# Top-32 attention with an MLP on one Trainium2 core: the smaller halves of the late score rows made by GpSimd as an integer difference

## The chip, the cores and the metric

The kernel runs on one core of one Trainium2 chip. That core has five instruction queues that matter here: TensorE (PE, matrix products), VectorE (DVE), ScalarE (ACT), GpSimd (POOL) and SyncE (SP, which issues the transfers). Each queue runs its instructions in the order in which the program put them; between queues there are only semaphores. The metric is the device time of one execution in microseconds (us).

## What is computed

Attention in which each query keeps only its 32 largest scores, followed by a layer norm and a two-layer MLP with a residual. Cut to what matters:

```python
# batch 8, heads 8, sequence 576, head size 64; all float32
scores = scale * np.matmul(q, k.transpose(0, 1, 3, 2))
kth = np.partition(scores, -32, axis=-1)[..., -32:-31]
scores = np.where(scores >= kth, scores, -1e9)
attn = softmax(scores)
x = heads_joined(np.matmul(attn, v))            # (8, 576, 512)
xn = (x - mean(x)) / np.sqrt(var(x) + 1e-6) * g_ln
out = x + np.maximum(xn @ w_ch1, 0.0) @ w_ch2   # 512 -> 2048 -> 512
```

## The kernel before

**Units.** The score rows are worked off in 160 units, numbered from 0. A whole unit has 128 queries of two heads: a tile `sc` of 128 partitions by two rows of 576 scores. There are 128 whole units. The other 32, called rest units, hold the last 64 queries of two heads in one row of 576.

**Finding the 32nd largest score of a row.** VectorE's MAX8 gives the eight largest of a row, and MATCH_REPLACE8 overwrites those eight, so four rounds give the threshold. To make these rounds shorter, `halve` (lines 442 to 457) first folds the row of 576 into two of 288: `hi` has the larger, `lo` the smaller of each pair (a score and the one 288 places further). Both were made by VectorE, in one TENSOR_TENSOR each (lines 456 and 457). `select` (line 459) then runs four rounds, 0 to 3, on `hi`; at the start of round 1 it takes the eight largest of `lo` (line 470) and puts them beside `hi`, so that rounds 2 and 3 also see them (296 elements). If more than eight of a row's 32 come out of `lo`, that is not enough: GpSimd's small subtraction in `watch` (line 497) records what is needed to notice it, and a second pass of the whole kernel would follow. It does not run with these inputs.

**What follows a unit.** `prepare` and `mask` (lines 486 and 524): ScalarE scales the threshold (line 490), makes a steep ramp of the row (RELU, line 527), and GpSimd subtracts the scores from it (line 530); the exponential on ScalarE (line 538) then gives zero outside of the 32. The weights are turned, for most units by VectorE's transpose (line 572) and a round trip through HBM, for others by PE (line 601), and PE multiplies them by the values (line 664). The MLP's products (lines 821, 860, 981) are cut into small items and handed out between these steps so that PE has work all the time. For most row blocks the second layer uses a seven-product scheme; its sums and differences are made by GpSimd (lines 911 to 917), as are the joins of its parts (961, 965), the residual (789) and the centring for the layer norm (743, 746).

**The order.** It is written out by hand in one loop over steps `n` (line 1265). In step `n` the current unit `u` is unit `n`, `nxt` is unit `n+1` and `mk` is unit `n-1`. In order of the code, a step does: scores of unit `n+2` on PE, masks of `mk` and its watch, the copy of the scores of `n+2` from PSUM (line 414), round 0 of `u`, MLP items, round 1 of `u` (with line 470), the transpose of unit `n-2`, rounds 2 and 3 of `u`, and last `halve(nxt)`. The calls `fill()` between them hand out MLP items, and with them the sums, joins and residuals that are due on GpSimd.

**Buffers.** `lo` has one buffer (`lopool`, line 70). `hi` has two fixed homes (line 110), taken in turn. `sc` has five. The first steps also convert the MLP's weights from their 64-bit form, on ScalarE, GpSimd and VectorE; `CONVERTING` (line 1103) is the last step of that, 21.

Of the kernel before, what the change touches and what calls it, by code (L numbers as in the profile page):

```python
# [10 lines left out]
ALU = mybir.AluOpType  # L11
FP32 = mybir.dt.float32
U32 = mybir.dt.uint32
# [16 lines left out]
def compute(  # L30
# [12 lines left out]
    nc = tc.nc  # L43
    P = nc.NUM_PARTITIONS
# [12 lines left out]
    def pool(name, bufs, **kw):  # L57
        return ctx.enter_context(tc.tile_pool(name=name, bufs=bufs, **kw))
# [3 lines left out]
    HALF = S // 2  # L62
# [7 lines left out]
    lopool = pool("lo", 1)  # L70
# [23 lines left out]
    def brief(name):  # L94

        return psps.tile([P, 512], FP32, tag="ps", name=name)
# [345 lines left out]
    def halve(u):  # L442

        nt = len(u.tiles)
        u.lo = lopool.tile([P, 2, HALF], FP32, tag="lo", name="lo")  # L450
        u.hi = hi_homes[u.i % 2]
        sides = int(doubt is not None)
        u.low, u.body = (sides * LOWS + HALF, sides * LOWS) if doubt is None or u.i // 2 % 2 else (0, LOWS)
        a, b = u.sc[:, 0:nt, 0:HALF], u.sc[:, 0:nt, HALF:S]
        lo, hi = u.lo[:, 0:nt], u.hi[:, 0:nt, u.body : u.body + HALF]
        nc.vector.tensor_tensor(hi, a, b, ALU.max)  # L456
        nc.vector.tensor_tensor(lo, a, b, ALU.min)  # L457

    def select(u, i):

# [25 lines left out]
    def prepare(u):  # L486

        nt = len(u.tiles)
        u.bias, u.edge = u.top[:, 0:nt, 0], u.thr[:, 0:nt, 6]
        nc.scalar.mul(u.edge, u.thr[:, 0:nt, 7], STEEP)  # L490
        nc.scalar.mul(u.bias, u.bias, -scale)

    def watch(u):

        nt = len(u.tiles)
        half, c = u.i // 16 % 2, 1 + 2 * (u.i % 16)
        nc.gpsimd.tensor_tensor(
            watched[:, half, c : c + nt], u.hi[:, 0:nt, u.low + 7], u.thr[:, 0:nt, 7], ALU.subtract
        )
        if u.i % 16 == 15 or u.i == N - 1:  # L500
            u.ends_watch = True
            u.half = half
# [21 lines left out]
    def mask(u, t):  # L524
        if u.e is None:
            u.e = epool.tile([P, 2, S], FP32, tag="e", name="e")
        nc.scalar.activation(  # L527
            u.e[:, t], u.sc[:, t], AF.Relu, bias=u.edge[:, t : t + 1], scale=-STEEP
        )
        nc.gpsimd.tensor_tensor(u.e[:, t], u.e[:, t], u.sc[:, t], ALU.subtract)  # L530
# [21 lines left out]
    def heads_of(g, h, i0, i1):  # L552
        c0 = h * (J + 1)
        return g.pt[:, i0:i1, c0 : c0 + J]

    def ends_of(g, i0, i1):
        return g.pt[:, i0:i1, J]
# [101 lines left out]
    def values(g):  # L659
        vb = g.job.v  # L660
        av = brief("av")
        for c in range(J):
            for h in range(2):
                nc.tensor.matmul(  # L664
                    av[h * D : (h + 1) * D, 0 : g.nq],
                    vb[:, h * (J + 1) + c, :],
                    heads_of(g, h, 0, g.nq // 32)[:, :, c],
                    start=(c == 0),
                    stop=False,
                )  # L670
        for h in range(2):
            nc.tensor.matmul(  # L672
                av[h * D : (h + 1) * D, 0 : g.nq],
                ends[:, h * D : (h + 1) * D],
                ends_of(g, 0, g.nq // 32),
                start=False, stop=True,
            )
        g.av = av
# [345 lines left out]
    def form_pair(i, part):  # L1024

        lo, hi = slice(2 * i, 2 * i + 2), slice(NF // 2 + 2 * i, NF // 2 + 2 * i + 2)
        b11, b12 = w2[:, lo, 0 : 2 * P], w2[:, lo, 2 * P : DM]
        b21, b22 = w2[:, hi, 0 : 2 * P], w2[:, hi, 2 * P : DM]  # L1030
        tt = nc.gpsimd.tensor_tensor
        t1, t2 = wt[:, 0, lo], wt[:, 1, lo]
        if part == 0:
            tt(t1, b12, b11, ALU.subtract)
            tt(t2, b22, t1, ALU.subtract)
            return
        x = xpool.tile([P, 2, DM], FP32, tag="x", name="form")
        t4, t3 = (x[:, s].rearrange("p (f n) -> p f n", f=2) for s in range(2))
        tt(t3, t2, b11, ALU.subtract)
        tt(t4, b21, t2, ALU.subtract)  # L1040
        return i, x

    def keep_pair(made):
        i, x = made
        for s in range(2):
            nc.sync.dma_start(scratch[:, s, i], x[:, s])
        if i == 3:
            kept_forms[0] = now[0]
# [54 lines left out]
    CONVERTING = max(n for n in batches if batches[n]) + 2  # L1103
# [26 lines left out]
    for j in jobs:  # L1130
        if j.hp == NHP - 1:
            b = j.b
# [26 lines left out]
    def at(i):  # L1159
        return units[i] if 0 <= i < N else None  # L1160
# [96 lines left out]
    take_scores(units[0])  # L1257
    load(fresh[1], nc.sync, nc.scalar)
    halve(units[0])
    scores(units[1])  # L1260
    take_scores(units[1])
# [3 lines left out]
    for n in range(END):  # L1265
# [8 lines left out]
        u, nxt, mk = at(n), at(n + 1), at(n - 1)  # L1274
# [14 lines left out]
            scores(x)  # L1289
        if g and not quick:  # L1290
            values(g)
        if mk:
            prepare(mk)
            for t in range(len(mk.tiles)):
                mask(mk, t)
        if mk and doubt is not None:
            watch(mk)
        if all(map(done, ready)):
            if made_pair:
                keep_pair(made_pair.pop())  # L1300
            if pairs_left:
                made = form_pair(*pairs_left.pop(0))
                made_pair.extend([made] if made else [])
            if None not in (kept_forms[0], plain_done[0]) and formed[0] is None:
                formed[0] = n
# [93 lines left out]
        if nxt:  # L1399
            halve(nxt)  # L1400
# [30 lines left out]
@with_exitstack  # L1431
def kernel(
    ctx: ExitStack,
    tc: tile.TileContext,
    *operands: bass.AP,
):
    nc = tc.nc
    doubt = ctx.enter_context(tc.tile_pool(name="doubt", bufs=1)).tile(
        [1, 1], I32, tag="doubt", name="doubt"
    )  # L1440
    compute(tc, *operands, low_rounds=1, doubt=doubt[:])
    again = nc.values_load(
        doubt[:], min_val=0, max_val=1,
        skip_runtime_bounds_check_because="a comparison's result",
    )
    with tc.If(again > 0):
        compute(tc, *operands, low_rounds=2, doubt=None)
# [31 lines left out]
```

## Time and profile before

| What | us |
|---|---|
| Median of three executions (lowest, highest) | 1563.04 (1561.82, 1563.74) |
| The profiled execution's own time | 1566.49 |
| Span of its instructions in the profile | 1564.6 |

The profile is of one execution, 3.45 us above the median. In it, "busy" is the time in which an engine executes; a wait is put down to what ended it. Instructions that have no record of their own time, such as issuing a transfer, are not counted as busy. PE's products are pipelined and their ends are modelled, so a PE that is busy all the time may still not be at its highest rate. The "chain that ended last" is found by going back from the last instruction to what released each one.

### The profile page before, as it was taken

Reading aid. Unit: us, or ns where it says so; the run is one execution under the profiler, and the core shown is the slowest. Engines: PE = TensorE matmul, PEld = TensorE weight load, DVE = VectorE, ACT = ScalarE, POOL = GpSimd, SP = SyncE. Lnnn points to the kernel's source line nnn. Section 1 sums busy time; section 2 is a strip of 40 time slices with the busy share of each in tenths; the row PEclk is TensorE's granted clock in tenths of the full one; section 3 lists DMA queues with packets and bytes.
Section 4 is the critical chain, followed back from the end, with each engine's and each line's share of the span. In section 5 each row is a group of like instructions: output and inputs, shape, how many; then the busy total and the mean of one; then the engine's idle time right before and its main releaser. Section 6 shows DMA issues by size and latency. Waiting matters only on the chain.

```text
span 1564.6 us, 27256 instructions
## 1 busy us (share of the span) xinstructions
PE 1467.7 (94%) x8046; PEld 1108.0 (71%) x8046; DVE 1349.1 (86%) x3873; ACT 1075.5 (69%) x3085; POOL 941.2 (60%) x1302
## 2 busy tenths in 40 slices
PE   3678889999999899999999999999999999999997
PEld 2456447576787677778777777777777777788886
DVE  6998899899889998989988999999999999767000
ACT  5988777786777767777777776867677776554421
POOL 4757776756474666656656556565647475737524
PEclk7789989999999999999999999999999999999998
DMA  6634541567648774686744796666667567464511
GB/s 174 165 100 122 143 114 60 151 157 209 177 127 201 192 204 130 180 207 151 222 119 133 183 225 183 159 171 182 187 173 197 173 173 196 118 173 114 151 35 50
DMA packets 374776, 245.62 MB, mean 157 GB/s; under 512 B 255956, under 2 KB 343512, under 8 KB 374616
## 3 DMA queue, kind: packets, MB, share of 16 engines
q1 hardware_dynamic: 371048, 243.17, 57.9%
q8 instruction: 67, 1.10, 0.3%
q10 hardware_dynamic: 3568, 0.59, 0.3%
q14 instruction: 93, 0.76, 0.2%
HBM read 166.14 MB, written 77.53 MB: 156 GB/s over the span
## 4 chain that ended last, share of the span: by engine, by line
PE 52%; DVE 31%; ACT 5%; DMA 5%; POOL 4%; issue 2%; SPq 1%; DVEq 0%; POOLq 0%; ACTq 0%
PE hps L821 21%; PE ops L981 13%; DVE m L478 10%; DVE hi L464 8%; PE scps L433 6%; PE av L664 5%; DVE sc L572 3%; DVE lo L457 2%; DVE hi L456 2%; PE ops L860 2%; DVE hi L470 2%; PE tp L601 2%; POOL e L530 2%; DMA raw<-in_moe_w_ch_dram 1%; PE av L672 1%
## 5 line engine op out<-in xcount | busy, mean ns | idle before, releaser
L530 POOL TENSOR_TENSOR e<-e,sc 128x576 f32<-128x576 f32 x288 | 408.7, 1437 | 492.6 <-ACT e L527 437.7
L821 PE MATMUL hps<-xT,w 128*128 128x256 f32 x2304 | 542.0, 384 | 1.6 <-ACT xT L781 1.6
L821 PEld LDWEIGHTS hps<-xT,w 128*128 128x128 f32 x2304 | 423.4, 191 | 80.8 <-issue 25.9
L478 DVE MAX8 m<-hi 128x8 f32<-128x296 f32 (+1 forms) x1152 | 472.8, 446 | 1.2
L464 DVE MATCH_REPLACE8 hi<-m,hi 128x288 f32<-128x288 f32 (+1 forms) x864 | 378.0, 443 | 0.0
L981 PE MATMUL ops<-w,h 128*128 128x256 f32 x1280 | 306.9, 385 | 1.3 <-ACT o L946 1.3
L981 PEld LDWEIGHTS ops<-w,h 128*128 128x128 f32 x1280 | 235.0, 191 | 44.8 <-issue 13.4
L414 ACT COPY sc<-scps 128x288 f32<-128x288 f32 x576 | 189.1, 402 | 76.8 <-POOL e L530 56.0
L538 ACT ACTIVATE e<-e,m 128x576 f32<-128x576 f32 x288 | 225.4, 785 | 7.8 <-POOL e L530 5.8
L527 ACT ACTIVATE e<-sc,m 128x576 f32<-128x576 f32 x288 | 209.3, 769 | 0.0
L572 DVE STREAM_TRANSPOSE sc<-e 128x1152 f32<-128x1152 f32 x87 | 119.0, 1367 | 52.7 <-ACT e L538 46.2
L844 ACT ACTIVATE h<-hps 128x512 f32<-128x512 f32 x144 | 86.7, 602 | 111.0 <-PE hps L821 110.4
L664 PE MATMUL av<-pt,vb 128*64 128x256 f32 (+2 forms) x1280 | 150.8, 379 | 9.6 <-DMA pt<-turned 6.2
L664 PEld LDWEIGHTS av<-pt,vb 128*64 128x64 f32 x1280 | 82.2, 142 | 69.6 <-issue 20.7
L456 DVE TENSOR_TENSOR hi<-sc 128x576 f32<-128x576 f32 (+1 forms) x160 | 127.0, 794 | 3.0 <-ACT sc L414 3.0
L457 DVE TENSOR_TENSOR lo<-sc 128x576 f32<-128x576 f32 (+1 forms) x160 | 126.9, 793 | 0.0
L433 PE MATMUL scps<-kT,late_qT 64*128 64x288 f32 (+3 forms) x832 | 119.9, 407 | 0.0
L981 PE MATMUL ops<-wt,s 128*128 128x256 f32 x512 | 119.4, 383 | 0.0
L433 PE MATMUL scps<-kT,qT 64*128 64x288 f32 x512 | 95.1, 465 | 24.6 <-ACT pt L613 9.0
L470 DVE MAX8 hi<-lo 128x8 f32<-128x288 f32 x288 | 117.8, 445 | 0.0
L981 PEld LDWEIGHTS ops<-wt,s 128*128 128x128 f32 x512 | 94.7, 190 | 17.3 <-issue 4.1
L433 PEld LDWEIGHTS scps<-kT,late_qT 64*128 64x128 f32 (+1 forms) x832 | 69.0, 166 | 50.0 <-issue 20.2
(108 smaller groups left out, 1747.2 us busy)
## 6 DMA issues: line engine op xcount, KB each, us to landing
turned<-sc SPq DMA_DIRECT2D x87, 576.0 KB, 4.3
pt<-turned SPq DMA_DIRECT2D x348, 144.0 KB, 3.1
w<-forms SPq DMA_DIRECT2D x128, 256.0 KB, 4.8
vb<-in_v_dram SPq DMA_DIRECT2D x80, 288.0 KB, 4.3
raw<-in_moe_w_ch_dram SPq DMA_DIRECT2D x32, 512.0 KB, 4.7
kT<-kept SPq DMA_DIRECT2D x48, 288.0 KB, 3.8
kept<-kT SPq DMA_DIRECT2D x32, 288.0 KB, 3.7
kqin<-in_k_dram SPq DMA_DIRECT2D x116, 72.0 KB, 2.7
```

The lines of the kernel that those rows point to most:

```text
L414: nc.scalar.copy(u.sc[:, t, s * HALF : (s + 1) * HALF], u.made[s][t][:, 0:HALF])
L433: nc.tensor.matmul(ps[i * R : i * R + ql, o : o + width], qT[r, q0 : q0 + ql], kT[r, k0 : k0 + width], start=True, stop=True,)
L456: nc.vector.tensor_tensor(hi, a, b, ALU.max)
L464: nc.vector.match_replace(x, m[:, t, :], x, LOWEST)
L478: nc.vector.max(m[:, t, :], u.hi[:, t, r0 : r0 + width])
L527: nc.scalar.activation(u.e[:, t], u.sc[:, t], AF.Relu, bias=u.edge[:, t : t + 1], scale=-STEEP)
L530: nc.gpsimd.tensor_tensor(u.e[:, t], u.e[:, t], u.sc[:, t], ALU.subtract)
L538: nc.scalar.activation(u.e[:, t], u.e[:, t], AF.Exp, bias=u.bias[:, t : t + 1], scale=-scale, accum_out=g.den[:, col : col + 1],)
L572: nc.vector.transpose(blocks.rearrange("p (j c n) -> p j c n", j=ni, n=32), u.e[:].rearrange("p t n -> p (t n)").rearrange("p (c j k) -> p ...
L664: nc.tensor.matmul(av[h * D : (h + 1) * D, 0 : g.nq], vb[:, h * (J + 1) + c, :], heads_of(g, h, 0, g.nq // 32)[:, :, c], start=(c == 0), s ...
L821: nc.tensor.matmul(ps[0][:, side * N : (side + 1) * N], w1[:, c, f * P : (f + 1) * P], self.xT[:, c, 0:N], start=(c == 0), stop=(c == NC - 1),
L981: nc.tensor.matmul(bank[name][:, 0:Q], a(j), rhs, start=first and j == 0, stop=(j == G - 1), skip_group_check=not first,)
```

## The change

For whole units after step `CONVERTING`, that is unit 22 (the 23rd) and later, `halve` no longer makes `lo`. GpSimd makes it in two integer instructions on the bits of the scores: first the sum of the bits of both halves (`both_halves`), then that sum less the bits of the larger half (`less_larger`). Addition and subtraction wrap around at 32 bits, so what is left are the bits of the smaller half exactly. There are 106 such units. Rest units and the first 22 units are made as before.

In a step, `less_larger(u)` stands on GpSimd's queue ahead of the masks of `mk`, and `both_halves(nxt)` behind the watch of `mk`. The larger half stays on VectorE at the end of the step before.

```diff
@@ halve
         nt = len(u.tiles)
-        u.lo = lopool.tile([P, 2, HALF], FP32, tag="lo", name="lo")
+        if not by_difference(u):
+            u.lo = lopool.tile([P, 2, HALF], FP32, tag="lo", name="lo")
...
         nc.vector.tensor_tensor(hi, a, b, ALU.max)
-        nc.vector.tensor_tensor(lo, a, b, ALU.min)
+        if not by_difference(u):
+            nc.vector.tensor_tensor(lo, a, b, ALU.min)
+
+    def by_difference(u):
+
+        return doubt is not None and not u.rest and u.i > CONVERTING
+
+    def both_halves(u):
+
+        u.lo = lopool.tile([P, 2, HALF], FP32, tag="lo", name="lo")
+        a, b = (u.sc[:, :, c : c + HALF].bitcast(U32) for c in (0, HALF))
+        nc.gpsimd.tensor_tensor(u.lo[:].bitcast(U32), a, b, ALU.add)
+
+    def less_larger(u):
+
+        lo = u.lo[:].bitcast(U32)
+        hi = u.hi[:, :, u.body : u.body + HALF].bitcast(U32)
+        nc.gpsimd.tensor_tensor(lo, lo, hi, ALU.subtract)
@@ the loop over steps
         if g and not quick:
             values(g)
+        if u and by_difference(u):
+            less_larger(u)
         if mk:
             prepare(mk)
             for t in range(len(mk.tiles)):
                 mask(mk, t)
         if mk and doubt is not None:
             watch(mk)
+        if nxt and by_difference(nxt):
+            both_halves(nxt)
```

## Prediction

> **What bounds the kernel now.** I read the page first: the busy time of the engines, the chain that ended last, and the costliest groups.
>
> ```profile
> span 1564.6 us, 27256 instructions
> PE 1467.7 (94%) x8046; PEld 1108.0 (71%) x8046; DVE 1349.1 (86%) x3873; ACT 1075.5 (69%) x3085; POOL 941.2 (60%) x1302
> ...
> PE 52%; DVE 31%; ACT 5%; DMA 5%; POOL 4%; issue 2%; SPq 1%; DVEq 0%; POOLq 0%; ACTq 0%
> ```
>
> TensorE (PE) and VectorE (DVE) share the chain, and GpSimd (POOL) stands far behind. An average over stages can hide what limits each, so next comes the busy time in three stretches (columns: window, its length, then busy time and instructions of PE, PEld, DVE, ACT and POOL, the granted clock, DMA).
>
> ```profile
> 0.00:300.00 300.00, 235.21 (x1137) 152.11 (x1138) 262.33 (x766) 234.16 (x629) 200.84 (x212) 0.89 0.47 124
> 300.00:1300.00 1000.00, 982.30 (x5646) 748.06 (x5645) 966.44 (x2786) 731.44 (x2166) 603.65 (x876) 0.99 0.67 177
> 1300.00:1565.00 265.00, 250.15 (x1267) 207.82 (x1265) 120.32 (x324) 109.92 (x292) 136.67 (x216) 0.98 0.42 118
> ```
>
> In the 1000 us from 300 to 1300, PE is busy for 982 and DVE for 966: two full engines, and each hands work to the other within about one unit. Time taken off DVE alone can therefore be refused by PE. POOL has 396 us idle there. After 1300 PE alone carries the time. What the change touches in the long stretch (groups by line and shape):
>
> ```profile
> L530 POOL TENSOR_TENSOR e<-e,sc 128x576 f32<-128x576 f32 x208 | 294.9, 1435 | 359.3 <-ACT e L527 309.3 <-PE scps L433 21.7 <-DVE m L478 17.5
> L457 DVE TENSOR_TENSOR lo<-sc 128x576 f32<-128x576 f32 x88 | 73.1, 830 | 0.0
> L456 DVE TENSOR_TENSOR hi<-sc 128x576 f32<-128x576 f32 x88 | 73.0, 829 | 0.0
> L821 PE MATMUL hps<-xT,w 128*128 128x256 f32 x1536 | 363.9, 383 | 0.0
> L981 PE MATMUL ops<-w,h 128*128 128x256 f32 x946 | 230.6, 386 | 1.3 <-ACT o L946 1.3
> L981 PE MATMUL ops<-wt,s 128*128 128x256 f32 x384 | 90.5, 383 | 0.0
> ```
>
> POOL's idle time stands almost wholly in front of the mask subtraction (L530), where it waits for ScalarE (ACT). So POOL is idle at the start of a step and does the rest of its queue after the masks.
>
> **What is removed.** 106 of the 160 units are whole and come from the 23rd on; 88 of them lie in the long stretch. DVE loses one minimum (L457) for each: 73.1 us there. How much of it the kernel can use depends on PE. PE leaves 1000 - 982 = 18 us, the least that it can give. What it could give beyond that, were its matrix products packed, is bounded by the rate of the chain's last long run:
>
> ```profile
> 1501.64 27.63 PE hps L821 x128
> ```
>
> 27.63 / 128 = 0.216 us each, so the 2866 such products (1536 + 946 + 384) need 619 us, where they are credited with 363.9 + 230.6 + 90.5 = 685: another 66 us at most. The relief lies between 18 and 73 us. I take 40, near the middle, because most steps have such products to pack, but in small groups between other work.
>
> **What is added, and its price.** GpSimd gets two integer instructions of 128x576 per unit: the sum of both halves (both_halves), and that sum less the larger half (less_larger). The trace has no such instruction at this size. The nearest rows are the float subtraction of the same size (1435 ns above) and GpSimd's integer addition of 128x512:
>
> ```profile
> L178 POOL TENSOR_TENSOR w<-wt 128x512 uint32<-128x512 uint32 x20 | 25.1, 1277 | 0.0
> L178 POOL TENSOR_TENSOR w<-size,wt 128x512 uint32<-128x512 uint32 x12 | 17.8, 1492 | 3.5 <-DVE size L172 3.5
> ```
>
> Scaled by 576/512 these give 1.44 and 1.68 us. I take 1.41, one undisturbed float subtraction (its row is shown below), as the lower integer row agrees with it; the upper end is 1.68. So 88 x 2 x 1.41 = 248 us enter a stretch with 396 idle: POOL goes from 604 to some 852 of 1000. It has room on average. What matters is when. The next rows are one whole step on DVE, from one larger half to the next, and then POOL in the step after it.
>
> ```profile
> 377.85 1.16 DVE L457 TENSOR_TENSOR lo<-sc 128x576 f32<-128x576 f32 x1
> 378.94 0.81 DVE L478 MAX8 m<-hi 128x8 f32<-128x288 f32 x2
> ...
> 380.15 0.44 DVE L464 MATCH_REPLACE8 hi<-m,hi 128x288 f32<-128x288 f32 x1
> 380.51 0.80 DVE L470 MAX8 hi<-lo 128x8 f32<-128x288 f32 x2
> ...
> 385.15 0.73 DVE L456 TENSOR_TENSOR hi<-sc 128x576 f32<-128x576 f32 x1
> 385.81 0.74 DVE L457 TENSOR_TENSOR lo<-sc 128x576 f32<-128x576 f32 x1
> ...
> 388.06 0.80 DVE L470 MAX8 hi<-lo 128x8 f32<-128x288 f32 x2
> ...
> 394.02 0.73 DVE L456 TENSOR_TENSOR hi<-sc 128x576 f32<-128x576 f32 x1
> ```
>
> ```profile
> 386.76 2.78 POOL L530 TENSOR_TENSOR e<-e,sc 128x576 f32<-128x576 f32 x2 [3.59 <-ACT e L527]
> 389.50 0.20 POOL L497 TENSOR_TENSOR watched<-hi,m 128x2 f32<-128x2 f32 x1
> 389.65 3.36 POOL L917 TENSOR_TENSOR h<-h,s 128x128 f32<-128x128 f32 x8
> 393.09 0.19 POOL L756 TENSOR_SCALAR rstd<-mv 128x2 f32<-128x2 f32 x1
> 393.37 0.71 POOL L759 TENSOR_TENSOR rstd<-rstd,columns 128x2 f32<-128x2 f32 x1
> ```
>
> The new waits. In the changed order POOL issues, in each step: less_larger, the two masks, the watch, both_halves for the next unit, and only then the rest (sums of the hidden rows, residuals, centring). less_larger waits for L456; DVE's L470, which picks the eight largest of lo, waits for less_larger; both_halves waits for that L470, as lo has one buffer. Between the end of L456 and L470 DVE has two MAX8 and two replacements: 380.51 - 378.94 = 1.57 us. One GpSimd instruction of 1.41 plus two handshakes just fits. A wait of zero holds only while POOL is free at that moment; each microsecond by which it is late, DVE stands still, with the rest of the selection, the moves (L572) and the next larger half queued behind.
>
> In the step shown POOL has 2.78 + 0.20 + 3.36 + 0.19 + 0.71 = 7.2 us of work. With 2.8 more it is 10.0, against a DVE step of 394.02 - 385.15 = 8.87 less 0.66 (385.81 - 385.15, the pitch of the two halves). So here POOL arrives 1.8 us late. I went through the 88 whole units in this way: POOL's instructions per step as the changed program orders them, with the durations of these rows, against DVE's own work in that step, lateness carried over. In 29 of them POOL is over 0.2 us late, and the lateness sums to 52 us; the steps are those with a burst of eight L917, with two triples of sums, with a residual, or the first whole unit after the short remainder units. PE sets about half of the chain, and lateness in those places costs nothing: the low end is 26. With 1.68 us for each instruction there are 88 x 2 x 0.27 = 48 us more of POOL work, so the high end is about 100. I take 40: most late steps are short ones in which DVE has no slack.
>
> **The shared read of VectorE and GpSimd.** Two rows, one of each engine, show that L456 can wait for a GpSimd instruction:
>
> ```profile
> 800.67 1.41 POOL L530 TENSOR_TENSOR e<-e,sc 128x576 f32<-128x576 f32 x1 [5.67 <-PE scps L433]
> 800.86 1.84 DVE L456 TENSOR_TENSOR hi<-sc 128x576 f32<-128x576 f32 x1
> ```
>
> The clean larger half takes 0.73; here it starts 0.19 after the mask and takes 1.84, so it ended only after the mask had. On average 0.83 - 0.73 = 0.10 us per half are lost so. The change takes one of two such halves away and makes POOL busier at the other: 88 x 0.10 = 9 us gone (inside the 73), about as much more at L456, which I cost at nothing; the ends are 9 us either way. The Trainium skill ("SBUF — State Buffer", section "Who interferes with whom") says that a DVE instruction with two SBUF inputs and a GpSimd instruction that reads SBUF exclude each other for the whole instruction, whichever comes first. By that rule the price could reach a whole GpSimd instruction for each larger half; these two rows agree with the exclusion, and the mean of 829 ns shows how rarely it bites today.
>
> **The masks move back.** less_larger stands ahead of the masks of the unit before. In some steps ACT's next copy of scores waits for these masks:
>
> ```profile
> ACT sc L414 <- POOL e L530: 56.0, 25, 4.4
> ...
> 1070.14 1.41 POOL L530 TENSOR_TENSOR e<-e,sc 128x576 f32<-128x576 f32 x1 [3.37 <-ACT e L527]
> ...
> 1071.59 0.70 ACT L414 COPY sc<-scps 128x288 f32<-128x288 f32 x2 [1.52 <-POOL e L530]
> ```
>
> ACT's copy starts 0.04 us after the mask's end; behind it on ACT stand the copies that free PSUM for PE. 25 times 1.41 is 35 us at most, 0 at least; ACT has 269 us free in the stretch, so I take 10.
>
> **Both ends.** Before 300 seven changed units meet the weight conversion's POOL work: the tally gives 9 us late against six or so saved. After 1300 DVE's saving is worth nothing, but the chain runs through POOL once:
>
> ```profile
> 1407.31 2.77 POOL e L530 x2
> ...
> 1416.71 2.44 POOL o L789 x2
> ```
>
> Two to three new instructions in such a place are 3 to 4 us. Together +8, between 0 and 20.
>
> **The sum.** -40 + 40 + 10 + 8 = +18 us on the profiled execution's 1566.49 (span 1564.6 and 1.9 around it), which is 3.45 above the median of the three runs, 1563.04. Against that median: 1581.
>
> **The rivals.** (1) *POOL's room suffices; faster.* For it: 396 us idle against 248 added, and 59 of 88 units with no lateness. Against it: PE at 982. Relief 55, lateness 26, nothing else: -29, or -20 with a little of the mask delay: 1534 to 1543. It decides if POOL reaches less_larger before L456 ends in nearly all steps. (2) *GpSimd becomes the bound.* Place: less_larger; price: 1.68 us per instruction, L470 late in most whole steps, since 1.57 no longer covers it. Lateness 100, masks 35, ends 20, relief 73: +82, 1645; with half of the excess 1615. It decides from about 1.5 us on, where even a free POOL makes DVE wait. The Trainium skill's "GPSIMD Engine Reference", section "4.1 Engine selection", sends two-input elementwise work to VectorE, GpSimd being about twice as slow; the rows (1435 against 829) agree. (3) *No change:* PE at 982 refuses the relief, and what DVE loses is what it was given: 1563.
>
> **How the numbers follow.** Forecast (slower by 0.2 to 2.7%, 1567 to 1605) 0.46; GpSimd as the bound 0.16; faster 0.29; no change 0.09. What can be told from no change is 0.2%, about 3 us. So slower 0.62. The range 1548 to 1620 leaves about 0.1 at either end: at the low end most of rival (1), at the high end the worse half of rival (2).
>
> **What would show it.** In the profile of the changed kernel: no L457 on 106 units; the two new lines at 1.38 to 1.45 us each (if 1.6 or more, rival 2); a new wait of DVE's L470 for POOL of 40 to 70 us in total, in some 30 units, where L470 waits for nothing today; POOL over 80% busy from 300 to 1300, with its wait for ACT's L527 fallen from 309 to under 150; ACT's L414 waiting longer for L530; PE's busy share of that stretch lower than 98%. I am wrong if L470 waits for under 20 us, or if PE stays at 98% while the stretch gets shorter.

## The result

The change made the kernel slower: 1648.73 us (1647.71 to 1651.05) against 1562.43 us (1561.69 to 1563.74) of the kernel before on the same chip, a ratio of 1.0553 with a 95% interval from 1.0535 to 1.0572. That is 86 us more, where the forecast had 18 and its range ended at 1620. The profiled execution took 1649.08.

### The profile page after: what moved, and what is told of

It is laid out like the page before. It is cut to its first block, busy times and chain, and to the rows that moved or that the text cites. A ratio compares the mean times of both kernels' runs of the same rounds, so it can differ in the third digit from the quotient of the medians.

```text
span 1647.3 us, 27523 instructions
## 1 busy us (share of the span) xinstructions
PE 1496.7 (91%) x8046; PEld 1121.0 (68%) x8046; DVE 1283.1 (78%) x3767; ACT 1074.8 (65%) x3085; POOL 1211.0 (74%) x1514
## 4 chain that ended last, share of the span: by engine, by line
PE 32%; DVE 30%; POOL 25%; ACT 4%; issue 4%; DMA 3%; SPq 1%; DVEq 0%; POOLq 0%; ACTq 0%
PE hps L842 15%; DVE hi L485 9%; DVE m L499 9%; PE ops L1002 8%; POOL lo L478 6%; POOL e L551 5%; DVE sc L593 3%; PE scps L433 3%; DVE hi L491 3%; PE av L685 3%; POOL lo L472 2%; DVE hi L457 2%; POOL h L938 2%; POOL o L810 1%; POOL s L933 1%
## 5 line engine op out<-in xcount | busy, mean ns | idle before, releaser
L551 POOL TENSOR_TENSOR e<-e,sc 128x576 f32<-128x576 f32 x288 | 403.4, 1419 | 207.5 <-ACT e L548 172.2
L842 PE MATMUL hps<-xT,w 128*128 128x256 f32 x2304 | 548.7, 387 | 1.6 <-ACT xT L802 1.6
L842 PEld LDWEIGHTS hps<-xT,w 128*128 128x128 f32 x2304 | 428.0, 193 | 82.8 <-issue 26.2
L499 DVE MAX8 m<-hi 128x8 f32<-128x296 f32 (+1 forms) x1152 | 477.6, 454 | 4.9
L485 DVE MATCH_REPLACE8 hi<-m,hi 128x288 f32<-128x288 f32 (+1 forms) x864 | 381.1, 451 | 0.0
L1002 PE MATMUL ops<-w,h 128*128 128x256 f32 x1280 | 313.0, 390 | 8.1 <-ACT o L967 7.1
L559 ACT ACTIVATE e<-e,m 128x576 f32<-128x576 f32 x288 | 225.3, 785 | 39.8 <-POOL e L551 37.6
L414 ACT COPY sc<-scps 128x288 f32<-128x288 f32 x576 | 188.0, 402 | 96.2 <-POOL e L551 80.9
L478 POOL TENSOR_TENSOR lo<-lo,hi 128x576 uint32<-128x576 uint32 x106 | 149.1, 1407 | 114.9 <-DVE hi L457 112.0
L485 DVE MATCH_VALUE_LOAD hi<-m,hi 128x8 f32 x864 | 74.1, 86 | 199.9 <-POOL lo L478 196.6
L472 POOL TENSOR_TENSOR lo<-sc 128x576 uint32<-128x576 uint32 x106 | 149.7, 1412 | 6.1 <-DVE hi L491 6.1
L511 ACT ACTIVATE m<-m 128x2 f32<-128x2 f32 (+1 forms) x160 | 32.8, 205 | 161.5 <-DVE m L499 161.3
L457 DVE TENSOR_TENSOR hi<-sc 128x576 f32<-128x576 f32 (+1 forms) x160 | 125.9, 787 | 3.0 <-ACT sc L414 3.0
L433 PE MATMUL scps<-kT,late_qT 64*128 64x288 f32 (+3 forms) x832 | 123.8, 414 | 3.4 <-ACT sc L414 3.4
L491 DVE MAX8 hi<-lo 128x8 f32<-128x288 f32 x288 | 118.6, 450 | 0.0
```

The source lines that it names most:

```text
L414: nc.scalar.copy(u.sc[:, t, s * HALF : (s + 1) * HALF], u.made[s][t][:, 0:HALF])
L433: nc.tensor.matmul(ps[i * R : i * R + ql, o : o + width], qT[r, q0 : q0 + ql], kT[r, k0 : k0 + width], start=True, stop=True,)
L472: nc.gpsimd.tensor_tensor(u.lo[:].bitcast(U32), a, b, ALU.add)
L478: nc.gpsimd.tensor_tensor(lo, lo, hi, ALU.subtract)
L485: nc.vector.match_replace(x, m[:, t, :], x, LOWEST)
L499: nc.vector.max(m[:, t, :], u.hi[:, t, r0 : r0 + width])
```

## The profile after

The page first, as before. Inserted lines move the numbers: the larger half is now L457, the eight largest of `lo` L491 (L470 before), the replacement L485 (L464), the picking of the eight largest of `hi` L499 (L478), the mask's subtraction L551 (L530). The new lines are L472 (both_halves) and L478 (less_larger).

```profile
span 1647.3 us, 27523 instructions
PE 1496.7 (91%) x8046; PEld 1121.0 (68%) x8046; DVE 1283.1 (78%) x3767; ACT 1074.8 (65%) x3085; POOL 1211.0 (74%) x1514
...
PE 32%; DVE 30%; POOL 25%; ACT 4%; issue 4%; DMA 3%; SPq 1%; DVEq 0%; POOLq 0%; ACTq 0%
```

VectorE lost 66 us of work and GpSimd gained 270. GpSimd's share of the chain that ended last rose from 4% to 25%, at the expense of TensorE, yet GpSimd is busy for only 74% of the span. An engine with a quarter of its time idle can thus carry a quarter of the chain: it is not full, it is late. The busy time in the stretches of the prediction (same columns; the last window is longer):

```profile
0.00:300.00 300.00, 234.08 (x1125) 152.07 (x1127) 247.77 (x737) 230.49 (x620) 212.53 (x222) 0.88 0.46 124
300.00:1300.00 1000.00, 935.21 (x5261) 704.78 (x5257) 854.49 (x2510) 676.66 (x2005) 769.39 (x975) 0.97 0.62 165
1300.00:1648.00 348.00, 327.44 (x1664) 264.17 (x1662) 180.84 (x522) 167.63 (x460) 229.04 (x318) 0.98 0.45 126
```

In the long stretch both engines that were full are now waiting: TensorE fell from 982 to 935 of 1000 and VectorE from 966 to 854. Where VectorE waits, its list of waits says (instruction, releaser, sum in us, how often, longest):

```profile
DVE hi L485 <- POOL lo L478: 196.6, 106, 15.8
```

All of it stands at the replacement L485, 106 times, once for each changed unit, and none at the read of `lo`. The groups by line:

```profile
L478 POOL TENSOR_TENSOR lo<-lo,hi 128x576 uint32<-128x576 uint32 x106 | 149.1, 1407 | 114.9 <-DVE hi L457 112.0
L485 DVE MATCH_VALUE_LOAD hi<-m,hi 128x8 f32 x864 | 74.1, 86 | 199.9 <-POOL lo L478 196.6
L472 POOL TENSOR_TENSOR lo<-sc 128x576 uint32<-128x576 uint32 x106 | 149.7, 1412 | 6.1 <-DVE hi L491 6.1
L491 DVE MAX8 hi<-lo 128x8 f32<-128x288 f32 x288 | 118.6, 450 | 0.0
```

L491 has 0.0 us of idle time before it. The reason stands in a line that the diff does not touch. less_larger reads `hi`; round 0's MATCH_REPLACE8 overwrites `hi` in place. So the replacement may not begin until less_larger has read the larger half: a write after a read. The step that the prediction shows, on VectorE and then on GpSimd:

```profile
400.26 0.75 DVE L457 TENSOR_TENSOR hi<-sc 128x576 f32<-128x576 f32 x1
401.05 0.82 DVE L499 MAX8 m<-hi 128x8 f32<-128x288 f32 x2
402.54 0.09 DVE L485 MATCH_VALUE_LOAD hi<-m,hi 128x8 f32 x1 [0.67 <-POOL lo L478]
...
403.40 0.81 DVE L491 MAX8 hi<-lo 128x8 f32<-128x288 f32 x2
```

```profile
401.09 1.41 POOL L478 TENSOR_TENSOR lo<-lo,hi 128x576 uint32<-128x576 uint32 x1 [0.73 <-DVE hi L457]
402.46 2.78 POOL L551 TENSOR_TENSOR e<-e,sc 128x576 f32<-128x576 f32 x2
...
406.72 3.87 POOL L938 TENSOR_TENSOR h<-h,s 128x128 f32<-128x128 f32 x8
...
411.63 1.41 POOL L478 TENSOR_TENSOR lo<-lo,hi 128x576 uint32<-128x576 uint32 x1
```

GpSimd was free here and had itself waited 0.73 us for the larger half. It began 0.04 us after VectorE's two MAX8 began and needs 1.41 where they last 0.82, so VectorE stands for 0.67. That is the best case: over all 106 units the shortest of these waits is 0.66 us, half of them are under 0.74, and the shortest taken 106 times is 70 us. It is as long as the minimum that was taken off VectorE (0.66 from one half to the next). In a unit in which GpSimd is on time VectorE therefore gains nothing. In the next step GpSimd is late as well: the second L478 begins at 411.63, when this row of VectorE says that the larger half was long done:

```profile
409.36 0.92 DVE L457 TENSOR_TENSOR hi<-sc 128x576 f32<-128x576 f32 x1
```

It ended at 410.28, so 1.35 us of lateness come on top, behind the eight L938 and what followed them.

## The experiments

Each ratio is to the kernel before, run on the same chip beside it, with its 95% interval. Where us are given for a ratio's difference, they are that difference times 1564.

### The replacement without its wait (e1)

The larger half gets a home of its own, `big`, that nothing overwrites; round 0 reads it and writes the replaced row into the other home. less_larger reads `big`. Compared with the changed kernel (cut to what matters):

```diff
-        u.hi = hi_homes[u.i % 2]
+        u.hi, u.big = hi_homes[u.i % 2 if doubt is None else 1], hi_homes[u.i % 2 if doubt is None else 0]
...
-        lo, hi = u.lo[:, 0:nt], u.hi[:, 0:nt, u.body : u.body + HALF]
+        lo, hi = u.lo[:, 0:nt], u.big[:, 0:nt, u.body : u.body + HALF]
...
-        hi = u.hi[:, :, u.body : u.body + HALF].bitcast(U32)
+        hi = u.big[:, :, u.body : u.body + HALF].bitcast(U32)
         nc.gpsimd.tensor_tensor(lo, lo, hi, ALU.subtract)
...
+        src = u.big if i == 0 else u.hi
...
-                replace(m, t, u.hi[:, t, r0 : r0 + width])
+                x = u.hi[:, t, r0 : r0 + width]
+                nc.vector.match_replace(x, m[:, t, :], src[:, t, r0 : r0 + width], LOWEST)
```

> The changed kernel, but the larger half goes to one of the two hi homes and round 0 writes its replaced copy to the other, so that GpSimd's second subtraction may still read the larger half while VectorE replaces. Same instructions on every engine, same buffers. Theory A (the wait moved to round 0's first replacement, because the subtraction still has to read what the replacement overwrites: at least 0.67 us in each of the 106 units, 71 us in all): the wait in front of the replacements (197 us) disappears, a wait of 60 to 100 us remains in front of the MAX8 of lo, and the time falls from 1649 to 1565 to 1600. Theory B (GpSimd's load and its lateness set the time, wherever VectorE waits for it): the wait moves to the MAX8 of lo nearly whole, over 150 us, and the time stays above 1625.

Measured: 1614.92 us, 1.0326 (1.0308 to 1.0344): between both. Its waits on VectorE:

```profile
DVE hi L491 <- POOL lo L478: 149.0, 62, 15.0
```

The wait at the replacement is gone, and with it 35.5 us (1.0553 - 1.0326). What is left stands where the prediction had put it, at the read of `lo`, in 62 of 106 units and with 149 us. The tally was of the stretch alone, 52 us in 29 of 88 units; of the 149 us, 90 in 45 units lie between 300 and 1300 of this run. So the overwriting is one cause, not the only one.

### The relief alone, and the load alone (e2, e3, e5 and again e2b, e5b)

e2 leaves the minimum out of the kernel before (`lo` is then a fixed tile with old values). e3 keeps it and gives GpSimd two stand-in integer additions of zero in the places of less_larger and both_halves, which nothing in the four rounds of the selection waits for. The larger half of a unit may still have to wait for them, since they write score rows that it reads. e5 is both.

```diff
# e2
-        nc.vector.tensor_tensor(lo, a, b, ALU.min)
+        if not by_difference(u):
+            nc.vector.tensor_tensor(lo, a, b, ALU.min)
# e3
+    def spend(row):
+        x = row.bitcast(U32)
+        nc.gpsimd.tensor_tensor(x, x, columns[:, 3:4].bitcast(U32).to_broadcast([P, S]), ALU.add)
...
+        if u and by_difference(u):
+            spend(u.sc[:, 0])
...
+        if nxt and by_difference(nxt):
+            spend((u if not u.rest else nxt).sc[:, 1])
```

> The kernel before without VectorE's minimum on the 106 units and with nothing in its place: round 1 reads a smaller half left by an earlier unit. It measures the relief by itself, which the prediction put at 40 us (18 to 73). If TensorE refuses most of it: 1540 to 1560. If VectorE alone bounds the kernel: 106 x 0.85 = 90 us less, 1473 to 1490.

> The kernel before with VectorE's minimum kept, and in the places of the two new GpSimd instructions two others of 128x576 (uint32 addition of zero, in place on one row of scores), for which nothing on VectorE waits in the selection. It measures GpSimd's load and the later masks alone. Theory A: 1563 to 1580. Theory B: above 1600.

> Both at once: the minimum left out (round 1 reads a smaller half left by an earlier unit), GpSimd's two instructions spent as in the run with the load alone, no handshake. Theory A: near the relief alone, at most 20 us above it, so 1540 to 1570; then all of the changed kernel's loss is the handshake. Theory B: above 1590.

e2 and e5 gave no usable time: the old values in `lo` started the kernel's second pass, and 3272.59 and 3291.44 us are two passes. Only a sign can be had from the first pass of each: the last join on GpSimd began at 1532.60 (e2) and 1553.43 (e5), against 1553.98 in the kernel before. e3 took 1605.06 us, 1.0258 (1.0241 to 1.0275), as theory B had it: GpSimd's load costs 40 us beside a VectorE that keeps its minimum. Some of that belongs to the stand-ins themselves: the larger half (L457 there) waits 21.8 us for them, 12 times. e2 and e5 were then run again with the flag of the second pass held at zero:

```diff
-        nc.vector.tensor_copy(doubt, w[0:1, P : P + 1])
+        nc.vector.tensor_copy(doubt, w[0:1, 8:9])
```

> The relief alone again (no minimum on the 106 units, round 1 reads a smaller half left by an earlier unit), with the flag that starts the second pass held at zero. In the earlier run the first pass ended 21 us sooner than in the kernel before (its last join began at 1532.6 against 1554.0). Expected: 1541 to 1546, so a relief of 17 to 24 us.

> Relief and GpSimd load without handshake again, with the flag held at zero. In the earlier run the last join of the first pass began at 1553.4, as in the kernel before. Expected: 1560 to 1568. Then the load costs about as much as the relief gives, and everything by which the changed kernel is above 1563 is the two waits of VectorE: about 50 us for lateness at the smaller half and 34 us for the replacement.

Measured: e2b 1545.36 us, 0.9889 (0.9867 to 0.9910); e5b 1564.59 us, 0.9998 (0.9987 to 1.0010). Both are where they were expected. The relief alone is worth 17 us (14 to 21), about the smallest value that the prediction allowed. The window from 300 to 1300 of e2b points to what refuses the rest:

```profile
300.00:1300.00 1000.00, 991.82 (x5743) 758.34 (x5742) 935.90 (x2757) 743.79 (x2200) 608.08 (x888) 1.00 0.68 182
```

TensorE is at 992 of 1000. In e5b the stand-ins cost these 17 us again. They took 1154 ns on average, less than the real ones, but the larger half waited 27.6 us for them (16 times), which it does not do in the changed kernel. So they bound the load from neither side; the next run takes the real instructions.

### The full load without a wait (e10)

GpSimd's two instructions are those of the change, but the subtraction reads the scores instead of `hi`, and L491 reads the first half of the scores instead of `lo`. Compared with the changed kernel (the flag is held at zero as above):

```diff
-        hi = u.hi[:, :, u.body : u.body + HALF].bitcast(U32)
+        hi = u.sc[:, :, 0:HALF].bitcast(U32)
         nc.gpsimd.tensor_tensor(lo, lo, hi, ALU.subtract)
...
-                    nc.vector.max(u.hi[:, t, o : o + 8], u.lo[:, t])
+                    nc.vector.max(u.hi[:, t, o : o + 8], u.sc[:, t, 0:HALF] if by_difference(u) else u.lo[:, t])
```

> The two instructions of the changed kernel at their full price (1.41 us; the earlier stand-ins took 1.15 to 1.19) in the same places, but VectorE's round 1 reads the first half of the row instead of the smaller half, and the subtraction reads the scores instead of the larger half: nothing on VectorE waits for GpSimd in the selection (the flag for the second pass is held at zero). Theory A (the handshake is the loss): 1562 to 1575. Theory B (with 300 us more of GpSimd work in an in-order queue the masks come late, and the loss of 50 us that stays without the replacement's wait is load): 1595 to 1615.

Measured: 1583.28 us, 1.0133 (1.0117 to 1.0148), between both again: 38 us above the relief alone. VectorE has no wait for GpSimd's two instructions left. GpSimd's wait for VectorE's larger half is gone as well (71.1 us in e1, none here), since the subtraction no longer reads that half; so this run frees GpSimd of a wait that the change has. Two costs show in the profile. The first is the masks, in ScalarE's waits of e10:

```profile
ACT sc L414 <- POOL e L551: 94.8, 25, 7.2
ACT e L559 <- POOL e L551: 57.3, 47, 3.8
```

In e2b the first of them is 54.0 us (25 times), and the second, of the exponential for the mask, 5.5 (11 times). The second is the sign that the masks now come late in many more places than the 25. The other cost is in the larger half on VectorE, by shape, in e10 and then in e2b:

```profile
L457 DVE TENSOR_TENSOR hi<-sc 128x576 f32<-128x576 f32 x128 | 146.0, 1141 | 3.0 <-ACT sc L414 3.0
```

```profile
L456 DVE TENSOR_TENSOR hi<-sc 128x576 f32<-128x576 f32 x128 | 112.8, 881 | 3.0 <-ACT sc L414 3.0
```

The same 128 instructions take 33 us more, and they meet a GpSimd instruction more often. In e2b 60 of them ran with no GpSimd instruction beside them for more than 0.06 us, in e10 only 24; these took 740 and 738 ns on average, the others 1006 and 1234. Part of this belongs to e10 alone: 12 of its larger halves began while less_larger was running, and they took 8 us more in sum than undisturbed ones. In the changed kernel this can't be, as less_larger waits for the larger half of its unit. How the 38 us divide between late masks and slower larger halves was not tried.

### Other places for less_larger (e7, e8)

Both start from e1. e7 makes the larger half of the next unit before round 2 of the current one and puts less_larger right behind it; e8 does the same two calls right behind round 0.

```diff
# e7
-        if u and by_difference(u):
-            less_larger(u)
...
+        if nxt and by_difference(nxt):
+            halve(nxt)
+            less_larger(nxt)
         if u:
             select(u, 2)
...
-        if nxt:
+        if nxt and not by_difference(nxt):
             halve(nxt)
# e8: the same two calls behind
             select(u, 0)
```

> The run with the larger half in its own home (1615), all 106 units, but VectorE makes the larger half of the next unit in the middle of the step (ahead of round 2) and GpSimd's second subtraction follows there, half a step before round 1 of the next unit needs it. Same instructions and load. Theory A: the wait for the smaller half falls from 149 to under 40 us and the time to that of relief and load without handshake, 1558 to 1580. Theory B (GpSimd's load by itself): the time stays above 1600.

> All 106 units, larger half in its own home, and VectorE makes the next unit's larger half right behind round 0 of the current one, so that GpSimd's second subtraction can stand behind the sum, ahead of the step's other GpSimd work (sums of hidden rows, joins, residuals, centring). The run before it, which only moved the larger half and left that other work ahead of the subtraction, still waited 144 us at the smaller half and took 1613. Theory A' (the place in GpSimd's queue makes the wait: the subtraction has until round 1 of the next step, and the other work no longer stands in front of it): the wait at the smaller half falls under 30 us, the time to 1560 to 1585, that is near the 1565 of relief and load without handshake. Theory B (GpSimd's load by itself, whatever the order): over 1600. In both the larger half may wait more for the masks, up to 0.7 us each.

Measured: e7 1613.31 us, 1.0318 (1.0298 to 1.0338), the same as e1; e8 1607.6 us, 1.0287 (1.0259 to 1.0316). The waits of VectorE in e7 and in e8:

```profile
DVE hi L491 <- POOL lo L478: 143.9, 56, 9.7
```

```profile
DVE hi L457 <- POOL lo L478: 84.1, 45, 8.0
DVE hi L491 <- POOL lo L478: 10.4, 9, 3.0
```

Theory A missed for e7: with two rounds of selection more for GpSimd to finish in, the wait was the same. In e8 the wait at the read of `lo` fell below 30 us as theory A' had it, but the time did not follow and came out on theory B's side. Most of the wait came back at the larger half L457, which may not be written while less_larger still reads the unit before (`big` has one buffer; a second was not tried). The two waits of e8 sum to 94.5 us, against 149.0 in e1, and its time is 6 us lower, little more than the uncertainty. So the lead moved most of the wait and shortened it by a third.

### Fewer units (e6, e9, e11)

e6 is e1 with the change left out of 42 units whose steps are heavy for GpSimd by the prediction's tally, so that 64 remain; e9 is e8 with those 64; e11 is e1 with the 32 units that have the most room, at least 2.6 us more work on VectorE than on GpSimd in their step. The rest have their minimum on VectorE, and all compute everything.

```diff
-        return doubt is not None and not u.rest and u.i > CONVERTING
# e6, e9
+        return doubt is not None and not u.rest and u.i > CONVERTING and u.i not in HEAVY
# e11
+        return doubt is not None and u.i in LIGHT
```

> The run with the larger half in its own home (1615), but the integer difference only on the 64 of the 106 units for which the tally of GpSimd's work finds it no more than 0.2 us late; the 42 others get VectorE's minimum. Theory A (lateness after a heavy step is the loss): waits for the smaller half below 30 us, time 1555 to 1575. Theory C (each handshake costs about the same, heavy step or not): 64/106 of the loss remains, 1595.

> The same order, but only on the 64 units that the tally found light. The 64-unit run with the subtraction at the top of the step took 1569. Theory A': the waits for the smaller half (31 us) go as well, 1552 to 1565; if load and relief go with the number of units, both cancel and it stays at 1560 to 1567, which would beat neither the kernel before by more than its spread.

> The larger half in its own home, and the integer difference only on the 32 units in whose step VectorE's own work exceeds GpSimd's by most (2.6 us or more by the tally). If relief and load go with the number of units and light steps hide the load: relief 32/106 of 19.5 = 6 us, so 1556 to 1562. If the load costs as much here as elsewhere: 1563 to 1567.

Measured: e6 1569.26 us, 1.0034 (1.0019 to 1.0050); e9 1575.13, 1.0081 (1.0051 to 1.0111); e11 1561.57, 0.9982 (0.9973 to 0.9991). The waits of VectorE and the long stretch of e11:

```profile
DVE hi L493 <- POOL lo L480: 10.0, 8, 4.0
DVE hi L493 <- POOL watched L522: 14.3, 10, 2.6
```

```profile
300.00:1300.00 1000.00, 984.96 (x5669) 748.63 (x5669) 959.94 (x2776) 735.66 (x2178) 691.64 (x938) 1.00 0.66 178
```

e6 is where theory A had the time, and its wait at `lo` is 31.0 us, just over the 30; the 1595 of theory C, the same price for every handshake, did not come. e9 missed: its waits for less_larger are down to 14.7 us at `lo` and 9.1 at the larger half, and still it is slower than e6, for a reason that was not tried. e11 is at the upper end of its first range. With 32 units in which GpSimd has room the wait for `lo` is down to 10.0 us, and TensorE is back at 985. e11 is the only version with the whole computation that is faster than the kernel before, by 2.8 us (0.18%), hardly more than can be told from nothing. The wait for `watched` belongs to the separate home of the larger half: the place for the eight of `lo` now comes round every second unit instead of every fourth. That layout alone, on the kernel before, was not tried.

## Why the prediction was wrong

The direction was right and the size far off. The runs build the 86 us up in four steps, each the difference of two ratios, so each is uncertain by some 3 to 4 us, and the four need not add up so neatly in another order (e3's load cost 40 us, e5b's similar one 17, and why they differ was not tried):

| step | runs | us | in the prediction |
|---|---|---|---|
| the minimum leaves VectorE | e2b | -17 | -40 |
| GpSimd's load, nobody in the selection waiting | e10 less e2b | +38 | +18 (masks 10, ends 8, shared read 0) |
| less_larger waits for VectorE's larger half, and L491 for a late GpSimd | e1 less e10 | +30 | +40 |
| the replacement waits for less_larger | after less e1 | +36 | none |

The third row is a net figure: e1 also has shorter larger halves than e10 (120.6 us against 146.0 in 128), so the waits alone may cost more than 30.

**The step that failed** is "DVE's L470, which picks the eight largest of lo, waits for less_larger", and with it "Between the end of L456 and L470 DVE has two MAX8 and two replacements: 380.51 - 378.94 = 1.57 us. One GpSimd instruction of 1.41 plus two handshakes just fits." I followed who reads the new result and not who overwrites what the new instruction reads. The first to wait is the replacement, and its cover is the two MAX8 alone, 0.82 us in the row above; 1.41 does not fit into it. So each of the 106 units waits, even with a free GpSimd. That costs 36 us, for which the sum has no term. Rival (2) came out near the measured time (1645, chance 0.16) by luck: its condition was 1.5 us or more for an instruction and a wait at L470, and neither came.

**Price of the instructions:** right. 1407 and 1412 ns stand against the 1.41 taken.

**Relief:** mis-sized. -17 against -40; the low bound of 18, what TensorE had left to give, was nearly the value, with TensorE at 992 of 1000. The credit for packing TensorE's products more tightly was not there to be had: in the stretch of e2b the products of L826 (L821 before) are credited with 374.3 us for 1582, 0.237 us each as before (363.9 for 1536). That TensorE refused the rest is read from its busy time, and not tried.

**Load without a wait:** mis-sized, 18 against 38. The masks were counted in the 25 places where the copy of scores waited before, but the exponential L559 waited too. In the changed kernel ScalarE's waits read:

```profile
ACT sc L414 <- POOL e L551: 80.9, 25, 5.8
...
ACT e L559 <- POOL e L551: 37.6, 39, 3.4
```

The shared read was costed at nothing, with 9 us either way. For the changed kernel itself that holds: its 128 larger halves take 110.6 us (864 ns each), before 109.6 (857). The 33 us more in e10 come up where VectorE does not wait for GpSimd; presumably it waits in the changed kernel in place of meeting GpSimd. That is argued, not tried.

**Lateness:** as a term of time near (30 against 40), but by luck, since two errors cancel. The waits of e1 are 90 us in the stretch where the tally had 52, and 59 more at both ends, where 9 were counted before 300 and none after 1300. And a microsecond of waiting was worth about a fifth of one in time (30 of 149) where I took most of it. The tally held every GpSimd instruction at its old length; why it came out so short was not tried.

**The signs.** No L457 for the minimum on 106 units, the new lines at 1.38 to 1.45, GpSimd's wait for the masks' ScalarE part down to under 150 in the stretch (68.4, from 309), L414 waiting longer (80.9, from 56.0) and TensorE under 98% (935 of 1000) all came. Two did not: GpSimd over 80% busy (769 of 1000), and 40 to 70 us of waits at L470. "I am wrong if L470 waits for under 20 us" is what happened: it waits for nothing, since the wait had been taken one instruction earlier.

## What to carry to other kernels

When one of two products moves to another engine, list who reads the new result and also who next overwrites what the new instruction reads; the cover is the work ahead of whichever comes first, here 0.82 us and not 1.57. The idle share of an in-order engine does not say that work fits in: some 300 us put on a GpSimd that was 60% busy cost 38 us with nobody waiting for the result, and only the version with the 32 units that have the most room in their step came out ahead, by 0.18%. Before crediting a relief, read how much the other full engine has left: TensorE had 18 us, and for 73 us taken off VectorE in that stretch the run became 17 us shorter.

## What the runs showed of the hardware

An integer subtraction of 128x576 on GpSimd costs what the float one does (1407 against 1419 ns in the changed kernel), and an integer addition with one value broadcast along the row costs less (1191 ns in e3, 1154 in e5b).

VectorE's larger half, which reads two halves of a row, takes longer when a GpSimd instruction runs beside it, though it waits for no result of it: 881 ns on average with GpSimd at 608 of 1000 us (e2b), 1141 with it at 840 (e10), where one that meets none takes 0.74 us. GpSimd's load alone does not set this mean: in e6 GpSimd is at 767 and the mean is 878. e10's stretch:

```profile
300.00:1300.00 1000.00, 972.72 (x5557) 735.78 (x5556) 936.89 (x2659) 719.36 (x2133) 840.13 (x1033) 0.99 0.65 174
```

The Trainium skill ("SBUF — State Buffer", section "Who interferes with whom") says that such an instruction and one of GpSimd that reads SBUF exclude each other for their whole length; the growth from 881 to 1141 ns agrees with it, without showing that the exclusion lasts so long.
